# Attention decode kernel (forward and backward): score rows in column strips for the second-batch heads that alternate with second-pass heads

## The chip, the cores and the metric

The kernel runs on one core of a Trainium2 chip. The metric is the device time in microseconds (us), the median of several runs of one program.

## The reference, cut to what matters

Two batch rows, 32 heads, one query token each, a cache of 8192 keys and values of width 128 per head. The forward pass is attention and a gated MLP with adaptive layer norm; the outputs are the result and the gradients of everything, of which dK and dV are by far the largest.

```python
q = (h @ wq).reshape(B, 1, 32, 128).transpose(0, 2, 1, 3)
scores = einsum('bhqd,bhkd->bhqk', q, k_cache) * 128 ** -0.5     # per head: 8192 scores
p = softmax(scores)
o = einsum('bhqk,bhkd->bhqd', p, v_cache)
out = x + gate * (o @ wo) ...                                     # then the MLP
# backward, per head: dV = p (outer) dO ;  dP = V dO ;  dS = p * (dP - sum) ;  dK = dS (outer) q
```

K and V of a head have 2.1 MB each. The kernel reads K once, V twice (once for the output, once for dP), and writes dK and dV: 671 MB of the 709 MB that it moves.

## The kernel before

A head of the *first pass* (A) is: load K and V, transpose K in blocks on TensorE, scores, maximum, exponent, scale K and take the products with V. A head of the *second pass* (C) is: load V again, transpose it, dP, and the two outer products on VectorE, each written out in two halves. Work is laid out in *slots*: a function put at a slot is emitted there, so slots fix the order of instructions on each engine, not the time. There are three stages. Heads 0 to 38 of the first pass follow each other, one per 8 slots (to about 450 us). Then 25 heads of the first pass (39 to 63, second batch) alternate with second-pass heads of the first batch, one pair per 16 slots, about 25 us: the **mixed stage**, up to about 1080 us. Then comes a **passage**, in which the MLP chain of the second batch is worked through, and the remaining second-pass heads, which end the kernel.

```python
    NHALF = 21                                   # big buffers, 1 MB each: half a head's K, V, dK or dV
    def htile():
        return halfp.tile([P, HK, P], BF16, name="half", tag="half")
    ...
    def transposes(block, dve):                  # 8 blocks of 128x128, and the copy out of PSUM
        tp = tps.tile([P, GRP, P], BF16, name="tp", tag="tp")
        for j in range(GRP):
            nc.tensor.transpose(tp[:, j, :], block(j), identb[:])
        kt = ktp.tile([P, GRP, P], BF16, name="kt", tag="kt")
        if dve: nc.vector.tensor_copy(kt[:], tp[:])          # groups 2 and 6
        else:   nc.scalar.copy(kt[:], tp[:])
        return kt

    def a_s(i, g):                               # scores of 8 blocks: K-transposed as weights, q as one column
        b, h = hb(i)
        kt = kts.pop((i, g))
        for j in range(GRP):
            cc = g * GRP + j
            nc.tensor.matmul(S_ps[i][:, cc:cc + 1], kt[:, j, :], qT_bf[:, h, b:b + 1], start=True, stop=True)
    ...
    def job_a(i, s):                             # NG = 8, LAG = 2, MOFF = 15
        for g in range(NG):
            at(s + g, PL_T, lambda g=g: a_t(i, g))
            at(s + g + LAG, PL_S, lambda g=g: a_s(i, g))
            at(s + g + MOFF, PL_M, lambda g=g: a_m(i, g))        # products with V
            at(s + g + MOFF, PL_FREE, lambda g=g: a_free(i, g))  # V halves free
        at(s + NG + LAG, PL_MAX, lambda: a_max(i))
        at(s + NG + LAG + 1, PL_MAX, lambda: a_bias(i))
        at(s + NG + LAG + 2, PL_EXP, lambda: a_exp(i))
        for q in range(NQ):
            at(s + NG + LAG + 3 + 2 * q, PL_TT, lambda q=q: a_scale(i, q))   # VectorE reads K
        ...
        at(s + MOFF + 2, PL_T, lambda: a_kp(i))                  # last matmul that reads K
        at(s + MOFF + 2, PL_FREE, lambda: k_free(i, 0))
        at(s + MOFF + 4, PL_FREE, lambda: k_free(i, 1))
        at(s + MOFF + NG, PL_EV, lambda: a_evac(i))
    ...
    def outer(store, dst, n, which, w2, q):      # dV and dK of the second pass
        hf, o = divmod(q * QK, HK)
        if o == 0:
            free["half"] -= 1
            store[(n, hf)] = htile()             # takes one of the 21 buffers
        ... nc.vector.tensor_tensor(... ALU.mult)
        if o + QK == HK:
            sq_.dma_start(src_of(dst, n)[:, hf * HK:(hf + 1) * HK, :], t[:])   # sq_ = nc.gpsimd
    ...
    # loads: nc.sync queue, in the order of the slot at which they are needed
    want(sA[i] + MOFF + hf * HG, lambda i=i, hf=hf: load_v(i, i, hf))
    ...
    A_END = end_a(sA[NHD - 1])                   # the passage is laid out from here
```

Every big tile takes one of the 21 buffers, and its first writer (a load on the SP queue, or VectorE's outer product) waits until the last user of the tile that was there before is done. The tile framework chooses the buffer when the program is built.

## Time and profile before

| | before |
|---|---|
| time, median of 3 runs | 1744.83 us (1744.82 to 1746.49) |
| bytes moved | 709.31 MB, 407 GB/s over the span |
| mixed stage, 480 to 1080 us | 413 GB/s, DMA share 1.01 |
| TensorE, VectorE, ScalarE busy there | 451.7, 410.5, 308.3 of 600 us |

Read a DMA-bound kernel by its rate, not by the busy share. The share is near 1.0 in nearly every window, at low rates as at high ones. (The Trainium skill, "Perfetto Trace Analysis", Identifying the Most-Contended Engine, says the same: bandwidth instead of occupancy. This trace agrees: a share of 1.01 at 413 GB/s, and still 0.98 at 384.) First, rows of the profile page's second part, 40 equal slices of the span: tenths of DMA's time busy, and GB/s.

```profile
DMA  9999999999999999999999999999999999999997
GB/s 381 417 417 418 418 417 389 418 378 398 375 417 422 418 410 422 411 404 414 409 410 412 420 407 394 369 415 420 425 421 421 410 411 395 417 416 415 410 411 319
```

The windows view of the kernel before follows: window in us; its length; busy us and instructions of TensorE, its weight loads, VectorE, ScalarE and GpSimd; granted clock; DMA share; GB/s.

```profile
20.00:400.00 380.00, 363.83 (x7504) 336.71 (x7505) 239.62 (x387) 228.16 (x321) 122.98 (x203) 0.98 1.01 409
480.00:1080.00 600.00, 451.70 (x8210) 424.66 (x8208) 410.53 (x514) 308.27 (x433) 138.50 (x236) 0.82 1.01 413
1080.00:1160.00 80.00, 63.42 (x1288) 60.18 (x1286) 61.27 (x126) 55.63 (x75) 13.56 (x24) 0.81 0.98 384
1240.00:1700.00 460.00, 346.52 (x4231) 269.61 (x4232) 298.07 (x322) 290.39 (x432) 58.97 (x111) 0.58 1.01 413
```

TensorE is nearly full in the first stage, has a quarter of its time free in the mixed stage, and the passage (third line) moves bytes at the lowest rate. Next, lines of the waits view of the kernel before, 480 to 1080 us: engine and line, for whom it waited, us in total, times, longest.

```profile
DVE half L1101 <- DMA out_dram<-half: 129.8, 23, 8.6
...
PE s_ps L386 <- DVE kt L369: 99.4, 22, 6.6
```

VectorE stood 129.8 us in the mixed stage because the buffer of an output tile was still being sent, and TensorE's score matmuls stood 99.4 us for a copy that VectorE had queued behind. The timeline of VectorE shows it in one period: the start, the length, the instruction, and in brackets the idle time before it and what ended it.

```profile
703.93 1.22 DVE L412 TENSOR_TENSOR ek<-half,e_15747 128x2048 bf16<-128x2048 bf16 x1
711.09 2.36 DVE L1101 TENSOR_TENSOR half<-Qr,ds_15957 128x2048 bf16<-128x2048 bf16 x2 [5.95 <-DMA out_dram<-half]
713.37 0.68 DVE L369 COPY kt<-tp 128x1024 bf16<-128x1024 bf16 x1
```

The first outer product of dK waits 5.95 us for an output transfer, and the copy of transposed K (kt) that TensorE needs comes after it. Last, the SP queue's own waits in that stage: the loads, too, wait for buffers that are being sent.

```profile
SPq L177 <- DMA out_dram<-half: 431.2, 48, 16.5
SPq L171 <- DMA out_dram<-half: 87.6, 22, 4.8
```

### The profile page before, as it was taken

Reading aid. Unit: us, or ns where it says so; the run is one execution under the profiler, and the core shown is the slowest. Engines: PE = TensorE matmul, PEld = TensorE weight load, DVE = VectorE, ACT = ScalarE, POOL = GpSimd, SP = SyncE. Lnnn points to the kernel's source line nnn. Section 1 sums busy time; section 2 is a strip of 40 time slices with the busy share of each in tenths; the row PEclk is TensorE's granted clock in tenths of the full one; section 3 lists DMA queues with packets and bytes.
Section 4 is the critical chain, followed back from the end, with each engine's and each line's share of the span. In section 5 each row is a group of like instructions: output and inputs, shape, how many; then the busy total and the mean of one; then the engine's idle time right before and its main releaser. Section 6 shows DMA issues by size and latency. Waiting matters only on the chain. (4 is left out here: it accounts for less than half of the span.)

```text
span 1743.7 us, 54710 instructions
## 1 busy us (share of the span) xinstructions
PE 1370.3 (79%) x24083; PEld 1221.6 (70%) x24083; DVE 1150.4 (66%) x1595; ACT 1008.0 (58%) x1431; POOL 371.9 (21%) x646
## 2 busy tenths in 40 slices
PE   6999999989967787686787778875577776785883
PEld 5999998879867676676776777875455555564672
DVE  2666666867876576577667668785566666675676
ACT  4666666646555545454454555696456555575784
POOL 0333333322221222222122123111011111110111
PEclk9999999989988878887888788698555556566577
DMA  9999999999999999999999999999999999999997
GB/s 381 417 417 418 418 417 389 418 378 398 375 417 422 418 410 422 411 404 414 409 410 412 420 407 394 369 415 420 425 421 421 410 411 395 417 416 415 410 411 319
DMA packets 109402, 709.31 MB, mean 407 GB/s; under 512 B 11175, under 2 KB 17683, under 8 KB 27243
## 3 DMA queue, kind: packets, MB, share of 16 engines
q1 hardware_dynamic: 67280, 421.59, 59.9%
q0 software_dynamic: 36864, 268.45, 37.0%
q10 hardware_dynamic: 5019, 15.78, 2.3%
q8 instruction: 188, 3.08, 0.7%
q14 instruction: 51, 0.42, 0.1%
HBM read 421.57 MB, written 284.20 MB: 405 GB/s over the span
## 5 line engine op out<-in xcount | busy, mean ns | idle before, releaser
L371 ACT COPY kt<-tp 128x1024 bf16<-128x1024 bf16 x794 | 800.9, 1020 | 546.4 <-PE tp L366 536.4
L366 PE MATMUL tp<-identb,half 128*128 128x128 bf16 x8192 | 772.7, 250 | 19.2 <-DVE kt L369 10.6
L366 PEld LDWEIGHTS <-half 128*128 128x128 bf16 x8192 | 599.8, 113 | 107.7 <-issue 94.6
L1106 POOL DMA_DIRECT2D out_dram<-half x256 | 136.2, 532 | 1034.3 <-DVE half L1101 883.0
L427 PE MATMUL m_ps<-ek,half 128*128 128x129 bf16 x4096 | 328.6, 223 | 1.1 <-DMA half<-in_A_v_cache_dram 1.1
L1078 PE MATMUL s_ps<-DO_bf,kt 128*128 128x1 bf16 x4096 | 192.5, 168 | 109.8 <-DVE kt L369 101.8
L1078 PEld LDWEIGHTS <-kt 128*128 128x128 bf16 x4096 | 186.3, 108 | 125.2 <-DVE kt L369 111.8
L369 DVE COPY kt<-tp 128x1024 bf16<-128x1024 bf16 x230 | 157.9, 686 | 153.6 <-PE tp L366 153.1
L386 PE MATMUL s_ps<-qT_bf,kt 128*128 128x1 bf16 x4096 | 177.7, 164 | 101.3 <-DVE kt L369 99.4
L427 PEld LDWEIGHTS <-half 128*128 128x128 bf16 x4096 | 248.9, 98 | 1.4 <-DMA half<-in_A_v_cache_dram 1.2
L386 PEld LDWEIGHTS <-kt 128*128 128x128 bf16 x4096 | 159.7, 98 | 106.2 <-DVE kt L369 103.6
L1230 ACT CAST stg<-m_ps 128x512 bf16<-128x512 f32 (+2 forms) x124 | 72.4, 584 | 68.5 <-PE m_ps L1229 68.4
L449 PE MATMUL k_ps<-half,pz 128*32 128x512 bf16 x1024 | 68.2, 386 | 23.0 <-POOL pz L435 23.0
L1229 PE MATMUL m_ps<-half 2*128 2x512 bf16 (+2 forms) x124 | 73.8, 595 | 1.2 <-ACT half L1204 1.2
L449 PEld LDWEIGHTS <-pz 128*32 128x32 bf16 x1024 | 21.9, 96 | 45.1 <-POOL pz L435 26.0
L1204 ACT CAST half<-m_ps 2x512 bf16<-2x512 f32 (+1 forms) x36 | 19.9, 564 | 34.9 <-PE m_ps L1201 34.4
L398 DVE TENSOR_REDUCE nm<-s_ps 128x1 f32<-128x128 f32 x64 | 18.4, 287 | 19.4 <-PE s_ps L395 19.4
L395 PE MATMUL s_ps<-nident,rm 128*128 128x128 bf16 x64 | 15.5, 243 | 19.4 <-DVE rm L390 19.4
L1312 ACT COPY kt<-tp 128x1024 bf16<-128x1024 bf16 x28 | 30.1, 1081 | 0.2
L1306 PE MATMUL tp<-identb,half 128*128 128x128 bf16 x224 | 20.3, 245 | 4.7 <-ACT kt L371 4.6
L488 DVE COPY OK<-m_ps 128x1 f32<-128x1 f32 x64 | 9.8, 154 | 20.5 <-ACT half L487 18.8
L729 PE MATMUL s_ps<-d_attn_bf,kt 128*128 128x1 bf16 x256 | 11.2, 165 | 14.8 <-ACT kt L718 12.1
(871 smaller groups left out, 1757.9 us busy)
## 6 DMA issues: line engine op xcount, KB each, us to landing
out_dram<-half POOLq DMA_DIRECT2D x256, 1024.0 KB, 13.7
half<-in_A_v_cache_dram SPq DMA_DIRECT2D x252, 1024.0 KB, 12.4
half<-in_A_k_cache_dram SPq DMA_DIRECT2D x128, 1024.0 KB, 19.6
out_dram<-stg ACTq DMA_DIRECT2D x22, 512.0 KB, 10.0
half<-in_A_wq_dram SPq DMA_DIRECT2D x8, 1024.0 KB, 10.2
half<-in_A_wo_dram SPq DMA_DIRECT2D x4, 1024.0 KB, 20.5
half<-in_w_mod_dram SPq DMA_DIRECT2D x3, 1024.0 KB, 15.9
half<-in_B_w_dram SPq DMA_DIRECT2D x3, 1024.0 KB
```

The source lines that it names most:

```text
L366: nc.tensor.transpose(tp[:, j, :], block(j), identb[:])
L369: nc.vector.tensor_copy(kt[:], tp[:])
L371: nc.scalar.copy(kt[:], tp[:])
L386: nc.tensor.matmul(S_ps[i][:, cc:cc + 1], kt[:, j, :], qT_bf[:, h, b:b + 1], start=True, stop=True)
L427: nc.tensor.matmul(m[:, 0:P + 1], vb_(i, kk), t[:, kk % QK, 0:P + 1], start=(kk == 0), stop=(kk == KK - 1), skip_group_check=True)
L449: nc.tensor.matmul(kp["ps"][NR * j:NR * (j + 1), :], pz[:, o:o + NR], K[(i, kk // HK)][:, kk % HK:kk % HK + QP, :], start=False, stop=(h = ...
L1078: nc.tensor.matmul(DP[n][:, cc:cc + 1], kt[:, j, :], DO_bf[:, b, h:h + 1], start=True, stop=True)
L1106: sq_.dma_start(src_of(dst, n)[:, hf * HK:(hf + 1) * HK, :], t[:])
L1229: nc.tensor.matmul(ps[:lw, 0:rw], rsl(ln, lc, lw, step), rsl(rn, rc, rw), start=True, stop=True)
L1230: nc.scalar.copy(st["t"][:lw, o:o + rw], ps[:lw, 0:rw])
L1306: nc.tensor.transpose(tp[:, j, :], rows[kc][:, (m0 + j) * P:(m0 + j + 1) * P], identb[:])
L1312: nc.scalar.copy(kt[:], tp[:])
```

## The change

The score matmuls of the 25 alternating heads are turned around. Instead of K-transposed as weights and the query as a single moving column (64 weight loads and 64 one-column matmuls a head), the query becomes the weights, padded with zeros so that one column of a 32-column strip holds it, and K-transposed moves, 512 columns at a time, in four strips side by side: 16 matmuls a head. The scores then stand in rows; ScalarE copies them out and four fp32 matmuls turn them into the columns that softmax wants. To make room, everything after the scores but the last copy of the outputs comes one slot later for these heads, and the stage that follows is laid out one slot later.

```diff
+    ssel = cst.tile([P, NSL * NST], F32, name="ssel")            # picks rows back into columns
+    qz = [cst.tile([P, NR + NSL - 1], BF16, name=f"qz{k}") for k in range(NZ)]   # zeros around q
...
     def a_t(i, g):
         if g == 0:
-            S_ps[i] = head_ps()
+            if i in byrows:
+                nc.gpsimd.tensor_copy(qz[i % NZ][:, NSL - 1:NSL], qT_bf[:, h, b:b + 1])
+            else:
+                S_ps[i] = head_ps()
...
+    def a_srow(i, g):
+        if g % SG < SG - 1:
+            return
+        a = g // SG
+        if a == 0:
+            R_ps[i] = mtps()
+        w = qz[i % NZ][:, NSL - 1 - a:NSL - 1 - a + NR]
+        for j in range(NST):
+            kt = kts[(i, g - SG + 1 + j * SW // GRP)]
+            o = j * SW % GRP
+            nc.tensor.matmul(R_ps[i][NR * j:NR * (j + 1), :], w, kt[:, o:o + SW, :],
+                             start=(a == 0), stop=(a == NSL - 1))
+    def a_rows(i):
+        t = ekp.tile([P, SW * P], F32, name="srow", tag="ek")
+        nc.scalar.copy(t[:], R_ps.pop(i)[:])
+    def a_cols(i):
+        S_ps[i] = head_ps()
+        for c in range(SW):
+            nc.tensor.matmul(sv[:, c, :], t[:, c * P:(c + 1) * P], ssel[:], start=True, stop=True)
...
     def job_a(i, s):
+        x = 1 if i in byrows else 0
+        MOFF = moff(i)                                            # MOFF + 1 for byrows
-        at(s + NG + LAG, PL_MAX, lambda: a_max(i))
+        if x:
+            at(s + NG + LAG, PL_EXP, lambda: a_rows(i))
+            at(s + NG + LAG + 1, PL_EXP, lambda: a_cols(i))
+        at(s + NG + LAG + x, PL_MAX, lambda: a_max(i))            # bias, exp, scale likewise + x
...
+    byrows.update(i for i in range(NHD) if sA[i] >= E0)           # heads 39 to 63
-    A_END = end_a(sA[NHD - 1])
+    A_END = end_a(sA[NHD - 1]) + 1
-            want(sA[i] + MOFF + hf * HG, ...load_v)
+            want(sA[i] + moff(i) + hf * HG, ...load_v)
```

Left out: the copy of one output column moves from VectorE to ScalarE for these heads, and two small uses of PSUM (the memory that matmuls write to) move to another bank, since the strips need one.

**What the diff does not say.** The later slot changes the moment at which K's buffers are given back, and with it the framework's choice of buffers. By the two built programs, ten big tiles take their buffers in each period of the mixed stage as follows (in 16 to 21 of 21 periods; 0 and 1 are halves; W is V loaded again for the second pass):

```
new tile   takes the buffer of, before      takes the buffer of, after
dK0        dV1  (an output transfer)        K0   (read last by TensorE)     <- swapped
V1         K0   (read last by TensorE)      dV1  (an output transfer)       <- swapped
W0 <- dK0   V0 <- dK1   K0 <- dV0   K1 <- V0   dV0 <- V1   dV1 <- W0   dK1 <- K1   W1 <- W1   in both
```

Below, this table is called the *handover*.

More of the change, by code (lines that the diff above doesn't have):

```diff
@@ L123 @@
     nc.vector.memset(pz[:], 0.0)
+    SW = 512 // P
+    NSL = KK // (SW * NST)
+    SG = SW * NST // GRP
+    ssel = cst.tile([P, NSL * NST], F32, name="ssel")
+    nc.vector.tensor_copy(ssel[:].rearrange("p (x j) -> p x j", j=NST),
+                          identb[:].rearrange("p (j x) -> p x j", j=NST)[:, 0:NSL, :])
+    NZ = 3
+    qz = [cst.tile([P, NR + NSL - 1], BF16, name=f"qz{k}") for k in range(NZ)]
+    for z in qz:
+        nc.vector.memset(z[:], 0.0)
     rsum = cst.tile([P, NHD], F32, name="rsum")
@@ L355 @@
     S_ps = {}
+    R_ps = {}
     M_ps = {}
@@ L376, in a_t @@
     def a_t(i, g):
+        b, h = hb(i)
         if g == 0:
-            S_ps[i] = head_ps()
+            if i in byrows:
+                nc.gpsimd.tensor_copy(qz[i % NZ][:, NSL - 1:NSL], qT_bf[:, h, b:b + 1])
+            else:
+                S_ps[i] = head_ps()
         kts[(i, g)] = transposes(lambda j: kb_(K, i, g * GRP + j), g in (2, 6))
+    byrows = set()
+    def a_srow(i, g):
[10 more added lines that the diff above has]
+                             start=(a == 0), stop=(a == NSL - 1))
+        for k in range(SG):
+            kts.pop((i, g - k))
+    def a_rows(i):
+        t = ekp.tile([P, SW * P], F32, name="srow", tag="ek")
+        nc.scalar.copy(t[:], R_ps.pop(i)[:])
+        kts[("row", i)] = t
+    def a_cols(i):
+        S_ps[i] = head_ps()
+        t = kts.pop(("row", i))
+        sv = S_ps[i][:, 0:KK].rearrange("p (m c) -> p c m", c=SW)
+        for c in range(SW):
+            nc.tensor.matmul(sv[:, c, :], t[:, c * P:(c + 1) * P], ssel[:], start=True, stop=True)
     def a_s(i, g):
+        if i in byrows:
+            return a_srow(i, g)
         b, h = hb(i)
@@ L487, in a_evac @@
         nc.scalar.copy(mstate[b][:, h, :], m[:, 0:P])
-        nc.vector.tensor_copy(OK[:, i, 0:1], m[:, P:P + 1])
+        if i in byrows:
+            nc.scalar.copy(OK[:, i, 0:1], m[:, P:P + 1])
+        else:
+            nc.vector.tensor_copy(OK[:, i, 0:1], m[:, P:P + 1])
     def job_a(i, s):
+        x = 1 if i in byrows else 0
+        MOFF = moff(i)
         for g in range(NG):
@@ L495, in job_a @@
             at(s + g + MOFF, PL_FREE, lambda g=g: a_free(i, g))
-        at(s + NG + LAG, PL_MAX, lambda: a_max(i))
-        at(s + NG + LAG + 1, PL_MAX, lambda: a_bias(i))
-        at(s + NG + LAG + 2, PL_EXP, lambda: a_exp(i))
+        if x:
+            at(s + NG + LAG, PL_EXP, lambda: a_rows(i))
+            at(s + NG + LAG + 1, PL_EXP, lambda: a_cols(i))
+        at(s + NG + LAG + x, PL_MAX, lambda: a_max(i))
+        at(s + NG + LAG + x + 1, PL_MAX, lambda: a_bias(i))
+        at(s + NG + LAG + x + 2, PL_EXP, lambda: a_exp(i))
         for q in range(NQ):
-            at(s + NG + LAG + 3 + 2 * q, PL_TT, lambda q=q: a_scale(i, q))
+            at(s + NG + LAG + x + 3 + 2 * q, PL_TT, lambda q=q: a_scale(i, q))
         at(s + MOFF, PL_EXP, lambda: a_pz(i))
@@ L507, in job_a @@
             at(s + MOFF + 4, PL_M, lambda: a_kp_out(i))
-        at(s + MOFF + NG, PL_EV, lambda: a_evac(i))
+        at(s + MOFF + NG - x, PL_EV, lambda: a_evac(i))
     def take_m(b):
@@ L512, in take_m, with moff @@
         free["half"] -= 1
+    def moff(i):
+        return MOFF + (1 if i in byrows else 0)
     def end_a(s):
@@ L1013 @@
         s += NG
-    A_END = end_a(sA[NHD - 1])
+    byrows.update(i for i in range(NHD) if sA[i] >= E0)
+    R0 = min([sA[i] for i in byrows], default=sA[NHD - 1])
+    A_END = end_a(sA[NHD - 1]) + 1
     CS1 = A_END + 1
@@ L1039 @@
                 want(sA[i] + hf * HG, lambda i=i, hf=hf: load_k(i, hf))
-            want(sA[i] + MOFF + hf * HG, lambda i=i, hf=hf: load_v(i, i, hf))
+            want(sA[i] + moff(i) + hf * HG, lambda i=i, hf=hf: load_v(i, i, hf))
     for b in range(B):
@@ L1081, in c_spread @@
         b, h = hb(n)
-        ps = mtps()[:, 0:2 * P]
+        ps = scr(2 * P) if R0 <= now[0] <= A_END else mtps()[:, 0:2 * P]
         nc.tensor.matmul(ps[:, 0:P], Qr_bf[:, b, h:h + 1].to_broadcast((P, P)), identb[:], start=True, stop=True)
@@ L1154, in task_dq @@
     def task_dq(b):
-        ps = mtps()
+        ps = scr(H)
         bs = slice(b * H, (b + 1) * H)
```

## The prediction

> **What bounds the kernel.** The page's DMA row is at 9 tenths in all slices but the last (7), 709.31 MB at 407 GB/s. The windows view splits it: first-batch stage (20-400 us) 409 GB/s, TensorE busy 363.8; mixed stage (480-1080 us, where a second-batch head alternates with a second-pass head) 413 GB/s, DMA share 1.01, TensorE busy only 451.7 of 600, VectorE 410.5, ScalarE 308.3; passage (1080-1160) 384; last stage 413. Windows of 4 us reach 424 to 432 GB/s at best. So the DMA engines bound the mixed stage, and TensorE has about a quarter of it idle: the waits view gives 99.4 us of score matmuls waiting for VectorE's copy, which itself stood 129.8 us behind output transfers whose buffers it needed.
>
> **What it removes and adds**, for 25 heads (39 to 63):
> - TensorE: 64 single-column score matmuls a head go (in the timeline, 8 advance it 0.21 us at full clock, so 1.7 us a head, 42 us in all). Added: 16 matmuls 128x512 into 32-row strips. k_ps has the form: 386 ns each, but 16 in about 1.0 us (the Trainium skill, "TensorE: Matmul & The Clock Gate", Part 3, says distinct column groups run concurrently; the trace agrees), and four fp32 matmuls (8 such take 0.86 us now), 0.4 us. Net gain, an estimate: 0.3 us a head, 8 us of idle engine.
> - ScalarE: one 128x512 copy (592 ns, as kprow) and the OK copy: about 0.75 us a head, 19 us. VectorE loses 25 x 0.157 = 4 us. One slot more lies between scores and outputs, so K is held longer.
>
> **The larger effect is indirect.** Comparing the buffer assignment of the two built programs: before, the first output tile of each second-pass head in the mixed stage reuses a buffer whose output transfer was issued six allocations ago, so VectorE blocks (5.95 and 6.74 us in two periods), TensorE stalls about 5 us, then all runs in a burst, after which the rate drops to 315-401 GB/s for some 4-8 us. After, that tile takes the buffer of a K half freed by TensorE; the waits for output transfers go to loads on the SP queue. VectorE's waits for output transfers in the mixed stage should nearly vanish, TensorE's stall with it; SP's wait for them should grow.
>
> The bytes are the same, all queues share the same 16 DMA engines (the Trainium skill, "Trainium Kernel Development and Optimization", Key Constraints), and their share is full, so unblocking VectorE can only fill the dips. At 424 GB/s throughout, the mixed stage would be 600 x (1 - 413/424) = 16 us shorter. I take under half: -7 us, and +1 us for the later slot.
>
> **Predicted: 1738 us; 8 in 10 between 1722 and 1752. Faster by over 2%: 5%; within 2%: 92%; slower by over 2%: 3%.**
>
> **Signs.** Right: mixed stage still DMA share about 1.01, at 415 to 420 GB/s; VectorE waits for output transfers in that stage under 40 us (129.8); TensorE's waits on VectorE's kt under 40 us; strips matmul 16 in about 1.0 us; last stage unchanged within 3 us. Wrong: DMA share under 0.98 in the mixed stage, or TensorE waiting for loads at over 2 us a period.
>
> **What would make it wrong.** (a) Loads now stand in order behind output transfers; if they come late, DMA starves and the stage is 1 us a period slower, +24 us. (b) A head's last scale now stands between the halves of the first output tile and delays it by 1.2 us. (c) The dips vanish wholly: -16 us, and more with the passage (7 us to give).

## The result, and the profile after

The changed kernel took 1746.25 us (median of 4 runs, 1743.93 to 1747.08) beside 1745.16 us before (1744.82 to 1746.49). The ratio is 1.0003, with a 95% interval of 0.9985 to 1.002. A ratio is the mean time of one kernel's runs over that of the other's in the same rounds, so it is not quite the ratio of the medians. A second set of five rounds on another chip gave a ratio of 1.0000 (0.9987 to 1.0013). There is no gain.

The lines of the profile after that answer to those above: first the page's rows.

```profile
GB/s 381 416 416 416 417 416 388 416 380 394 366 409 424 424 424 417 422 396 421 424 405 424 407 424 381 372 407 422 425 422 414 417 403 396 406 414 414 405 414 319
```

Then the windows view of the changed kernel, the same stages.

```profile
20.00:400.00 380.00, 364.08 (x7463) 337.33 (x7464) 238.14 (x383) 226.89 (x319) 123.36 (x203) 0.97 1.01 407
480.00:1080.00 600.00, 479.44 (x7314) 414.65 (x7314) 416.63 (x491) 319.94 (x483) 88.87 (x258) 0.85 1.01 415
1080.00:1160.00 80.00, 69.21 (x1269) 65.97 (x1268) 61.00 (x124) 54.52 (x75) 12.62 (x23) 0.70 0.99 380
1240.00:1700.00 460.00, 340.44 (x4194) 265.47 (x4194) 294.11 (x318) 290.03 (x432) 57.92 (x109) 0.58 1.01 411
```

The mixed stage is at 415 GB/s in place of 413; the passage is at 380 in place of 384 and the last stage at 411 in place of 413. Next, the waits view of the changed kernel in the mixed stage.

```profile
PE tp L377 <- DMA half<-in_A_k_cache_dram: 67.2, 25, 7.2
...
PE s_ps L423 <- ACT srow L415: 25.2, 24, 1.1
...
DVE half L1160 <- DMA out_dram<-half: 3.4, 1, 3.4
```

VectorE's 129.8 us behind output transfers are 3.4 us, as forecast. TensorE now waits 67.2 us for loads of K, 25 times, which the prediction had named as a sign against it if it came to more than 2 us a period; over the 24 periods it came to 67.2 / 24 = 2.8 us. The second line belongs to the new work: 25.2 us of TensorE standing for ScalarE's row copy. The loads on the SP queue wait for output transfers somewhat less than before, 472.8 us in place of 518.8, where the prediction had said that this should grow:

```profile
SPq L187 <- DMA out_dram<-half: 370.7, 68, 15.7
SPq L181 <- DMA out_dram<-half: 102.1, 22, 5.0
```

The timelines of VectorE and then TensorE of the changed kernel, in a comparable period. VectorE goes through the outer product of dK without a wait, with a head's last scale (ek) between its two halves. On TensorE, four strips take 0.34 us until the next instruction (0.33 to 0.34 in this period); the four fp32 matmuls are eight instructions, 0.91 us, after 1.05 us of waiting for the row copy; and a transpose waits 5.49 us for K.

```profile
704.25 1.22 DVE L1160 TENSOR_TENSOR half<-Qr,ds_15547 128x2048 bf16<-128x2048 bf16 x1
705.39 1.22 DVE L458 TENSOR_TENSOR ek<-half,e_15376 128x2048 bf16<-128x2048 bf16 x1
706.52 1.22 DVE L1160 TENSOR_TENSOR half<-Qr,ds_15547 128x2048 bf16<-128x2048 bf16 x1
```

```profile
709.48 0.40 PE L408 MATMUL m_ps<-kt,qz_108 128*32 128x512 bf16 x4
709.82 0.62 PE L377 MATMUL tp<-identb,half 128*128 128x128 bf16 x8
...
711.67 1.06 PE L423 MATMUL s_ps<-ssel,srow 128*128 128x16 f32 x8 [1.05 <-ACT srow L415]
712.58 0.61 PE L377 MATMUL tp<-identb,half 128*128 128x128 bf16 x8
...
722.36 1.04 PE L377 MATMUL tp<-identb,half 128*128 128x128 bf16 x8 [5.49 <-DMA half<-in_A_k_cache_dram]
```

So in TensorE's own order a head costs it more than before, not less: minus 8 x 0.21 = 1.7 us, plus 4 x 0.33 = 1.3 us of strips, 0.9 us of turning and 1.05 us of waiting.

**Where the trace gains and loses.** Adding up the rates of 4 us windows gives the time at which a trace has moved a given number of bytes. The table shows that time for the kernel before, and how much earlier (negative) or later the others are. The columns to the right of the first two are from experiments told below; each column is one execution, the profiled one. That of the kernel before took 1745.59 us, 1.2 to 2.9 us more than its medians beside the experiments (1742.67 to 1744.39), so the leads look larger by about that much than they are in the kernel's time. A second trace with the handover of before (e_double, below) stands 1.3 us ahead at 420 MB and 1.4 at 700.

| MB moved | before, us | changed | changed, second profile | best version | p_late | k_late |
|---|---|---|---|---|---|---|
| 200 (early in the mixed stage) | 496.8 | +2.9 | +0.3 | +0.8 | +1.2 | +1.5 |
| 320 | 785.8 | +1.0 | -3.1 | -3.9 | -4.1 | -3.3 |
| 420 (way into the passage) | 1028.8 | -2.3 | -7.7 | -7.6 | -7.8 | -6.1 |
| 460 | 1132.0 | -2.1 | -6.2 | -5.9 | -4.0 | -2.9 |
| 500 | 1227.6 | -0.9 | -5.1 | -5.3 | -4.2 | -2.7 |
| 700 (near the end) | 1711.2 | +1.5 | -4.3 | -4.2 | -2.1 | -2.6 |

The first profile of the changed kernel gained 5.2 us between 200 and 420 MB, but lost 2.9 us on the way in and 3.8 us on the way out. Its second profile, from the fastest of five runs (1741.09 us; the other four took 1743.8 to 1745.4), reached the forecast 7 us by the end of the mixed stage and gave back 3.4 us of it. The gain is in the mixed stage; the question is what takes it back.

### The profile page after: what moved, and what is told of

Its sections match the earlier page's. It is cut to its first block, busy times and chain, and to the rows that moved or that the text cites. A ratio compares the mean times of both kernels' runs of the same rounds, so it can differ in the third digit from the quotient of the medians.

```text
span 1745.0 us, 52735 instructions
## 1 busy us (share of the span) xinstructions
PE 1403.7 (80%) x23083; PEld 1216.6 (70%) x23083; DVE 1155.7 (66%) x1574; ACT 1018.3 (58%) x1481; POOL 318.7 (18%) x671
## 4 chain that ended last, share of the span: by engine, by line
issue 30%; PE 30%; DMA 28%; POOL 4%; DVE 4%; ACT 2%; SPq 1%; POOLq 0%; ACTq 0%; DVEq 0%
DMA half<-in_A_k_cache_dram 19%; PE tp L377 12%; PE m_ps L473 9%; DMA out_dram<-half 6%; POOL out_dram L1165 4%; PE k_ps L495 2%; PE s_ps L432 2%; DVE ek L458 2%; DVE half L1160 1%; DMA half<-in_w_mod_dram 1%; ACT kt L382 1%; PE m_ps L408 1%; DMA half<-in_A_wo_dram 1%; PE s_ps L423 1%; DMA half<-in_A_v_cache_dram 1%
## 5 line engine op out<-in xcount | busy, mean ns | idle before, releaser
L377 PE MATMUL tp<-identb,half 128*128 128x128 bf16 x8192 | 753.8, 247 | 79.1 <-DMA half<-in_A_k_cache_dram 69.0
L473 PE MATMUL m_ps<-ek,half 128*128 128x129 bf16 x4096 | 342.5, 228 | 4.0 <-DVE ek L458 2.3
L1137 PEld LDWEIGHTS <-kt 128*128 128x128 bf16 x4096 | 180.3, 106 | 122.0 <-DVE kt L380 105.5
L432 PE MATMUL s_ps<-qT_bf,kt 128*128 128x1 bf16 x2496 | 107.6, 164 | 1.0 <-DVE lnst L1020 0.4
L432 PEld LDWEIGHTS <-kt 128*128 128x128 bf16 x2496 | 96.8, 97 | 1.7 <-issue 1.0
L423 PE MATMUL s_ps<-ssel,srow 128*128 128x16 f32 x200 | 27.4, 269 | 25.2 <-ACT srow L415 25.2
L423 PEld LDWEIGHTS s_ps<-ssel,srow 128*128 128x128 f32 x200 | 24.9, 195 | 27.3 <-ACT srow L415 27.3
L1365 PE MATMUL tp<-identb,half 128*128 128x128 bf16 x224 | 20.4, 245 | 13.4 <-DVE kt L380 8.8
```

Source lines behind the costliest of these rows:

```text
L423: nc.tensor.matmul(sv[:, c, :], t[:, c * P:(c + 1) * P], ssel[:], start=True, stop=True)
L473: nc.tensor.matmul(m[:, 0:P + 1], vb_(i, kk), t[:, kk % QK, 0:P + 1], start=(kk == 0), stop=(kk == KK - 1), skip_group_check=True)
L1137: nc.tensor.matmul(DP[n][:, cc:cc + 1], kt[:, j, :], DO_bf[:, b, h:h + 1], start=True, stop=True)
```

## The experiments

Sixteen kernels were run in four sets; in each, the kernels shared a chip and the runs of the kernel before. The theories, at the outset: **A**, the dips in the mixed stage come from the handover of buffers, and the changed handover is worth some microseconds, which something else in the change costs again; **B**, the transfers cannot do better in that mix, so there was nothing to gain; and **C**, TensorE's time counts, and the strips cost what the handover gains.

### What the transfers alone can do

```diff
-    (all compute; this cut is shortened, four writes of zeros are left out)
+    def head_c(n):
+        for hf in range(2):
+            t = load(A_v_cache, n, hf)          # nc.sync, 21 buffers
+            store(t, out_3, n, hf)              # nc.gpsimd, from the loaded tile
+            store(t, out_2, n, hf)
+    for i in range(39): head_a(i)               # head_a loads K and V
+    for k in range(25): head_c(k); head_a(39 + k)
+    for n in range(25, 64): head_c(n)
```

> The big transfers alone (671 of the 709 MB: K, V, V again, and two outputs per head sent from the loaded V tile), in the same order of heads, through the same queues and 21 buffers, no compute, a wrong result on purpose. If the dips below 424 GB/s in the mixed stage come from how the engines hand over buffers (theory A, that of the prediction), this holds about 424 GB/s in every stage: 671.1 MB / 424 GB/s = 1583 us, and no stage below 420. If the transfers themselves cannot do better in the mix of reads and writes (rival B: nothing was there to gain), its mixed stage shows about 413 to 416 GB/s as in both kernels and the whole takes about 1620 us.

Measured: 1600.56 us (2 runs; of the small outputs only some zeros are written). The windows view of this run, its three stages, with busy time of VectorE and GpSimd only:

```profile
20.00:390.00 370.00, 0.00 (x0) 0.00 (x0) 1.00 1.01 422
400.00:1010.00 610.00, 0.00 (x0) 51.62 (x98) 1.00 1.01 427
1010.00:1580.00 570.00, 0.00 (x0) 82.85 (x156) 1.00 1.01 421
```

In the mix of the second stage the transfers run at 427 GB/s, against 413 and 415 in the two kernels: 600 x (1 - 413/427) = 20 us were there to gain at most. Theory B falls for that stage. Whether the engines' own reading and writing of the tiles, absent here, takes a part of the 20 us was not tested. (The Trainium skill, "HBM Reference", Specifications, gives about 425 GB/s to a core that streams alone; 422 for reads only here agrees roughly, and the mix does slightly better.) In the last stage the transfers alone come to 421 GB/s on average and both kernels are at 411 to 413, so less is left there. The larger gap lies at the passage: from 1080 to 1160 us the transfers alone are still at 427 GB/s, the two kernels at 384 and 380. The forecast of 420 everywhere held; the total of 1583 us did not: it left out the slower start and end (170 GB/s in the first 4 us, 225 and less in the last 12) and took 424 for every stage.

### Does TensorE's time count?

```diff
-            nc.tensor.matmul(S_ps[i][:, cc:cc + 1], kt[:, j, :], qT_bf[:, h, b:b + 1], start=True, stop=True)
+            for _ in range(2 if sA[i] >= E0 else 1):
+                nc.tensor.matmul(S_ps[i][:, cc:cc + 1], kt[:, j, :], qT_bf[:, h, b:b + 1], start=True, stop=True)
```

> The kernel before, with each of the 64 score matmuls of heads 39 to 63 issued twice (1600 more matmuls, some 42 us of TensorE at full clock). If TensorE is off the critical path in the mixed stage, the time stays within 3 us of before. If TensorE time counts there, it grows by 20 to 42 us, and then the removal of the same matmuls in the change should have gained.

Measured: 1746.99 us beside 1743.86, ratio 1.0017 (1.0003 to 1.003). The windows view of the mixed stage shows that the added work was done, at an almost unchanged rate:

```profile
480.00:1080.00 600.00, 484.07 (x9734) 455.08 (x9732) 410.49 (x514) 309.09 (x434) 137.88 (x235) 0.84 1.01 412
```

TensorE is busy 32 us more than before. The 1600 matmuls, with the handover of before, cost 3 us and not 20 to 42. Score matmuls of TensorE are nearly free in that stage, so removing them could gain little.

### The later slot alone, and the strips alone

The slot alone: the kernel before with `x`, `moff(i)` and the `A_END + 1` of the change, and its own column scores. Its handover is that of the changed kernel. The strips alone: the changed kernel with these lines back (the cut leaves out the last copy of the outputs, whose slot stays the same). Maximum, bias and exponent stay one slot later, since the rows must be turned first.

```diff
-        MOFF = moff(i)
-            at(s + NG + LAG + x + 3 + 2 * q, PL_TT, lambda q=q: a_scale(i, q))
+            at(s + NG + LAG + 3 + 2 * q, PL_TT, lambda q=q: a_scale(i, q))
-        return MOFF + (1 if i in byrows else 0)
+        return MOFF
-    A_END = end_a(sA[NHD - 1]) + 1
+    A_END = end_a(sA[NHD - 1])
```

> The kernel before with its column scores, but with the timing of the change alone: maximum, exponent, scale and outputs of heads 39 to 63 one slot later. The built program hands buffers over as in the changed kernel (VectorE's output tiles no longer reuse buffers that wait for an output transfer). Theory A1: the handover is worth 3 to 7 us and the strips cost it again, so this is 3 to 7 us faster than before. Rival: the handover only moves waits (TensorE then waits for K loads) and the time stays within 2 us of before.

> The changed kernel's strips without the later slot for the outputs: the scores are taken by strips and turned, and the outputs stay at the slots of before; VectorE's output tiles again wait for output transfers. Theory A1 (the strips cost TensorE time where it is on the path, at the entry to the mixed stage, and the handover gains it back): 2 to 6 us slower than before. Rival: strips cost nothing, within 2 us of before.

Measured: the slot alone 1744.81 us (1739.72 to 1746.7), ratio 0.9997 (0.9984 to 1.0011): no gain, although its trace was 7.3 us ahead at 420 MB. The strips alone 1757.67 us (1756.92 to 1761.25), ratio 1.008 (1.0066 to 1.0094): 14 us slower, far more than either theory had said. By its built program the framework had chosen a third handover there: W0 takes W0's buffer and dV1 takes dK0's, so that two of VectorE's four output tiles wait for transfers. Its waits view in the mixed stage, VectorE and then the SP queue, and its windows view:

```profile
DVE half L1159 <- DMA out_dram<-half: 110.6, 41, 8.4
```

```profile
SPq L187 <- PE tp L377: 336.5, 50, 12.7
```

```profile
480.00:1080.00 600.00, 488.86 (x7120) 421.85 (x7119) 401.87 (x478) 310.08 (x463) 115.26 (x253) 0.81 1.01 405
```

Loads stood 336.5 us for a transpose that had to release the buffer, and the stage ran at 405 GB/s. Either the strips cost 14 us or this handover does. That cannot be told from these two runs, since each edit also moved the buffers.

### Choosing the handover by hand

To tell them apart, the buffers were taken out of the framework's hands: 21 pools of one buffer each, and a table that names the buffer of every big tile. The table is read from another built program. Instructions and their order stay as they are; the framework still puts in every wait.

```diff
-    halfp = ctx.enter_context(tc.tile_pool(name="halfp", bufs=NHALF))
+    halfs = [ctx.enter_context(tc.tile_pool(name=f"half{k}", bufs=1)) for k in range(NHALF)]
-        return halfp.tile([P, HK, P], BF16, name="half", tag="half")
+        return halfs[HMAP[key]].tile([P, HK, P], BF16, name="half", tag="half")
+    HMAP = {("K", 0, 0): 19, ("K", 0, 1): 18, ...}     # 664 entries
```

h_swap is the kernel before with the table of the slot-only kernel; h_back the changed kernel with the table of the kernel before; h_strips the strips-alone kernel with the table of the slot-only kernel. e_20 is a check of another kind: `NHALF = 20`.

> The kernel before, instruction for instruction, but each big tile is put by hand into the buffer that it had in the slot-only kernel. In the mixed stage this swaps two of ten handovers: the first dK tile takes the buffer of the K half that TensorE has freed (it was that of dV's second output transfer), and the second V load waits for that transfer instead. Theory A1 (the handover is worth 7 us in the mixed stage, and the later slot, which holds K longer, or something after it takes this back): VectorE's wait for output transfers there falls from 130 us to under 15 us, and the time is 3 to 8 us under before. Rival (the handover only moves the wait): within 2 us.

> The changed kernel, instruction for instruction, but each big tile in the buffer that it had in the kernel before. Theory A1 (strips and later slot cost about as much as the handover gains): VectorE waits for output transfers again (over 90 us in the mixed stage) and the time is 3 to 10 us over before. Rival (handover, strips and slot are all free of effect): within 2 us of before.

> The kernel with strips and the old slots, which was 14 us slower than before, with its big tiles put by hand into the buffers of the slot-only kernel. If its 14 us came from its handover (two of VectorE's four output tiles and a load behind transfers, SP waiting 336 us for transposes), they go: within 3 us of before. If they came from the strips' own work, it stays 10 to 16 us slower.

> The kernel before with 20 big buffers in place of 21; by the built programs 10 of them circulate in the mixed stage in place of 11. If that stage is held by the number of buffers (the transfers alone reach 427 GB/s there), it loses about a tenth of the in-flight work and the time grows by 20 to 60 us, all of it after 400 us... the first-batch stage, which has more free buffers, loses less than 3 us. If buffers are plentiful, the time stays within 4 us.

| run | time, us | beside before, us | ratio (95% interval) |
|---|---|---|---|
| h_swap | 1740.93 (1740.27 to 1741.35) | 1744.3 | 0.9980 (0.9967 to 0.9994) |
| h_back | 1795.15 (1791.28 to 1798.62) | 1744.3 | 1.0290 (1.0276 to 1.0304) |
| h_strips | 1741.56 (1738.2 to 1742.36) | 1744.3 | 0.9979 (0.9966 to 0.9993) |
| e_20 | 1751.8 (2 runs) | 1744.3 | 1.0042 (1.0023 to 1.006) |

Four things follow.

The other table alone, with every instruction of the kernel before, gains 0.2%, 3.5 us (h_swap). In 104 of its 664 entries the tile follows another tile in its buffer than in the kernel before: 46 of these are the swap, 12 an exchange of V0 and W1 in six periods, and 46 lie at the end of the mixed stage or after it. The trace puts the gain before those last 46 (0.6 us ahead at 200 MB, 5.7 at 420, 4.6 at 700); the exchange in six periods was not separated from the swap. The waits view of h_swap in the mixed stage shows the same exchange as the changed kernel: VectorE no longer waits, TensorE waits for K.

```profile
PE tp L377 <- DMA half<-in_A_k_cache_dram: 65.1, 25, 4.4
...
DVE half L1112 <- DMA out_dram<-half: 2.8, 2, 1.4
```

The strips cost nothing: with that handover they are at 0.9979, without them at 0.9980. The 14 us of the strips-alone kernel were its handover. With e_double this removes theory C.

The changed kernel with the handover of before is 51 us slower (h_back), five times the upper end of what was expected. The waits and the windows view of that run say why:

```profile
DVE half L1171 <- DMA out_dram<-half: 119.0, 22, 8.5
...
PE m_ps L484 <- DVE ek L469: 103.5, 20, 8.4
```

```profile
480.00:1080.00 600.00, 433.98 (x6794) 369.11 (x6791) 383.04 (x451) 297.20 (x446) 81.50 (x242) 0.87 0.98 387
```

One slot later, a head's last scale comes after the first outer product of dK on VectorE. When that outer product waits for a transfer, the scale waits behind it (in one period of this trace the outer product starts at 700.72 us, after 5.90 us of waiting, and the scale at 701.86), and TensorE's products with V wait for the scale, 103.5 us in all. The stage falls to 387 GB/s. That V's buffers then come free late, and the loads with them, is the likely link; the SP queue's waits do not show it, since they come to 541 us in the mixed stage as against 545 before. So with the later slot the old handover would have cost 51 us. The framework's choice of the new one saved the change, and that was luck: nobody had asked for it.

With ten circulating buffers in place of 11 the kernel loses 0.4%, 7.5 us, under the 20 to 60 expected. This run is no clean test of the number, because the program built with 20 buffers has a handover of its own (K0 takes K0's buffer, V1 takes V0's). Its trace is 0.5 us ahead of before at 420 MB and 7.6 us behind at 460: the loss falls on the way into the passage, none of it in the mixed stage. (The Trainium skill, "Perfetto Trace Analysis", Optimization Strategy, says that equal gaps repeating on the engine that should be saturated can mean too few buffers. Here the repeated dips were mended in part, 413 to 415 GB/s from 480 to 1080 us in h_swap, at an equal number of buffers.)

### With and without the later slot, on one chip

> The changed kernel once more, on the chip of the three below, so that they can be compared with it there: within 3 us of before, as its first four runs were (+0.5 us by the ratio).

> The changed kernel with its big tiles put by hand into the buffers of the slot-only kernel; that differs from its own choice in two periods of the mixed stage. If these odd periods cost it the gain, it is 3 to 5 us under before. If the later slot costs the gain (theory now), it stays within 2 us of the changed kernel.

> The candidate that beat both: strips, outputs at the old slots, the same handover as the run above it; so it differs from that run only in the later slot. Theory: 2 to 5 us under before again, and at least 2 us under the changed kernel with the same handover. If it is within 1 us of that one, the later slot costs nothing and the difference seen between chips was chance.

> The slot-only kernel with its own handover, but the last three heads at the old slots, so that the stage that follows is laid out where it was before. The slot-only kernel led by 7.3 us at 420 MB in its trace and lost 3 to 5 us of it by 500 MB. If the later slot costs at this passage, this keeps the lead: 3 to 6 us under before. If it costs in every period, or not at the passage, it is 0 to 2 us under before.

"best" is h_strips once more: strips, the old slots, the new handover. h_mid is the slot-only kernel with the last three heads and `A_END` at the old slots.

| run | time, us | ratio to before (95% interval) |
|---|---|---|
| after_again (the changed kernel) | 1744.56 (1741.09 to 1745.41) | 1.0000 (0.9987 to 1.0013) |
| h_after (the same, handover by hand) | 1745.19 (1742.35 to 1745.98) | 1.0001 (0.9989 to 1.0012) |
| best (h_after without the later slot) | 1740.11 (1739.32 to 1742.14) | 0.9976 (0.9964 to 0.9988) |
| h_mid | 1743.53 (1736.68 to 1747.8) | 0.9992 (0.9974 to 1.0009) |

The pair h_after and best differs only in the later slot: (1.0001 - 0.9976) x 1744 = 4.4 us, clear of the noise (the slowest of five runs of best took 1742.14 us, the fastest of h_after 1742.35). The later slot takes back what the handover gains. The odd periods of the changed kernel's own handover cost nothing that can be seen, nor do the 21 pools in place of one (h_after is as after_again). h_mid scattered over 11 us and decides nothing. The best version beats the kernel before in two sets on two chips, by 0.21 and 0.24%, and the changed kernel in the one set in which both ran.

### Which part of the later slot?

Four more kernels, all with the new handover by hand. p_late: best with only `A_END + 1`. p_early: the changed kernel with `A_END` back. k_late: best with only the last reading of K and K's release one slot later. m_late: best with only the products with V and V's release one slot later.

```diff
 p_late   +    A_END = end_a(sA[NHD - 1]) + 1
 p_early  -    A_END = end_a(sA[NHD - 1]) + 1     (back to end_a(sA[NHD - 1]))
 k_late   +        at(s + MOFF + 2 + x, PL_T, lambda: a_kp(i))       # and both k_free + x
 m_late   +            at(s + g + MOFF + x, PL_M, lambda g=g: a_m(i, g))   # and a_free + x
```

> The best version (strips, old slots, new handover) with only the stage after the mixed one laid out one slot later. If the later slot costs at this hand-on, it gives back 2 to 4 us of the best version's lead: 0 to 2 us under before. If not, 3 to 5 us under before, as the best version.

> The changed kernel with the new handover and the later slot, but the stage after the mixed one laid out where it was before. If the hand-on is what costs, 2 to 4 us under before. If not, within 1.5 us of before, as with the hand-on one slot later.

> The best version with only the row of K products and the release of K one slot later for heads 39 to 63. If holding K longer is what costs, it gives back 2 to 4 us: 0 to 2 us under before. If not, 3 to 5 us under before.

> The best version with only the output products and the release of V one slot later for heads 39 to 63. If it is the outputs' later slot that costs, it gives back 2 to 4 us: 0 to 2 us under before. If not, 3 to 5 us under before.

| run | time, us | beside before, us | ratio (95% interval) |
|---|---|---|---|
| p_late | 1743.3 (1741.82 to 1745.67) | 1742.67 | 1.0001 (0.9988 to 1.0014) |
| p_early | 1742.84 (1740.86 to 1743.33) | 1742.67 | 0.9994 (0.9982 to 1.0007) |
| k_late | 1742.45 (1740.54 to 1743.39) | 1742.67 | 0.9993 (0.9981 to 1.0006) |
| m_late | 1740.55 (1738.58 to 1741.43) | 1742.67 | 0.9980 (0.9967 to 0.9994) |

The outputs' later slot costs nothing that can be seen (m_late keeps the lead of best). The version best itself was not run in this set; m_late stands in for it. Against m_late, laying the passage out one slot later costs 3.7 us by the ratios (3.3 by the plain means) and so takes the whole lead by itself (p_late, 1.0001). Holding K one slot longer costs 2.3 us (2.0 by the plain means; k_late, 0.9993), which is less certain: its interval overlaps that of m_late. Undoing the passage alone recovers only 1 us (p_early), within the noise. So the parts do not add up. Two more parts, the last scale and the loads of V one slot later, were not varied by themselves. The windows view shows where p_late loses, mixed stage and then the way into the passage; the version "best" is given first, then p_late.

```profile
480.00:1029.00 549.00, 441.89 (x6734) 375.66 (x6734) 380.46 (x448) 292.88 (x441) 120.66 (x242) 0.86 1.01 420
1029.00:1132.00 103.00, 85.70 (x1509) 78.42 (x1506) 75.08 (x128) 59.56 (x90) 18.05 (x32) 0.77 0.96 378
```

```profile
480.00:1029.00 549.00, 436.26 (x6736) 367.85 (x6734) 379.94 (x449) 292.45 (x441) 121.17 (x242) 0.88 1.01 420
1029.00:1132.00 103.00, 83.46 (x1443) 77.09 (x1441) 72.65 (x125) 57.66 (x86) 18.04 (x32) 0.75 0.96 372
```

Both run the mixed stage at 420 GB/s. In the 103 us after it p_late moves 372 GB/s and best 378, about 0.6 MB less, or 1.6 us. By the table above the two are 1.9 us apart at 460 MB and 2.1 at 700, so nearly all that these two traces differ by arises there. In one trace each, that is an indication, not a proof: p_early, with the passage at the old slots, loses as much on the way in (6.4 us ahead at 420 MB, 2.1 at 460). Why one slot matters at the passage, when the DMA rate there is so low for all of them, stays open.

## Why the prediction was right or wrong

- *DMA bounds the mixed stage, TensorE has time to spare there.* Right. TensorE's score matmuls twice over cost 3 us (e_double), and the strips cost nothing at an equal handover.
- *The larger effect is the handover.* Right, and it is more than an effect: with the change's instructions the two handovers are 51 us apart (h_back beside before, h_after at 1.0001), and with the instructions of before, the new handover gains 3.5 us (h_swap).
- *VectorE's waits for transfers vanish, TensorE's stall on VectorE's copy with them.* Right: 129.8 to 3.4 us, and 99.4 us to nothing for the score matmuls. But *SP's wait for them should grow* was wrong: 518.8 to 472.8 us. The wait that came in its place is TensorE's for K, 67.2 us.
- *At 424 GB/s the stage would be 16 us shorter; "I take under half: -7 us".* The mechanism was right, the size held for the stage and not for the kernel. Of twelve profiles taken with the new handover, eleven stood 5.7 to 7.8 us ahead of before at 420 MB, the first profile of the changed kernel only 2.3 us. In the kernel's time the handover is worth 3.5 to 4.2 us (h_swap, h_strips, best). A part of the lead is lost after 420 MB, not at the same place in every version: best is 7.6 us ahead at 420 MB, 5.3 at 500 and 4.2 at 700; h_swap loses nothing on the way into the passage (5.7 at 420 and at 460 MB) and ends at 4.6. Why is not shown.
- *"and +1 us for the later slot".* This is the step that failed most. Measured on one chip, the later slot costs 4.4 us (h_after against best). The prediction priced it as 1 us. Two parts of it cost more than that, each alone: the passage laid out a slot later (3.7 us, p_late against m_late by their ratios) and K held a slot longer (2.3 us, k_late against m_late, less certain). The prediction named the second ("K is held longer") and priced neither.
- The sum, -3.5 to -4 us of handover, about 0 of strips, and +4.4 us of slot, is the measured zero. The two mis-sized terms, -7 and +1, each make up about half of the 6 us by which the forecast was off.
- *TensorE's net gain of 0.3 us a head.* Wrong in sign, without consequence: a head costs TensorE 1.6 us more in its own order, because the four fp32 matmuls are eight instructions and wait for the row copy. The forecast of 0.4 us for the four took "8 such take 0.86 us" from the kernel before, but those 8 were the instructions of four matmuls: 0.86 us was the figure for four, and 0.91 was measured. The 16 strips, forecast at 1.0 us, take 1.3 in groups of four.
- *Wrong if TensorE waits for loads over 2 us a period.* It did (2.8 us), and this was no sign of a slower stage: h_swap waits as long (65.1 us) and is faster. In h_swap the wait moved from VectorE to TensorE, and the kernel gained by it.

What stays open: how one slot at the passage, or K held one slot longer, costs what it does; why the mixed stage ran at 417 GB/s from 480 to 1029 us in the first profile of the changed kernel and at 420 in the second; why p_late and k_late do not add up; and where the remaining 7 GB/s to the 427 of the transfers alone are lost in the mixed stage, and 40 GB/s at the passage.

## What to carry to other kernels

In a kernel that is bound by transfers, ask of every tile whose buffer it takes: in the kernel before, VectorE stood 129.8 us for buffers that were still being sent, and with it the copies queued behind, for which TensorE stood 99.4 us. With the wait at a load instead, TensorE stood 65.1 us for K, and the kernel was 3.5 us faster (h_swap). A shift by one slot can change this choice without a line of the diff saying so, so read the buffers out of the built program, and to learn what an edit costs, fix the buffers by hand and vary one thing at a time. A gain in one stage counts only as far as the stages after it keep the lead: of 7.6 us at the end of the mixed stage, best kept 4.2.

## What the Trainium skill lacked or had wrong

- "Perfetto Trace Analysis", Optimization Strategy, names too little room (buffer count, tile sizes) as a possible cause of repeated bubbles. It lacks another cause: which tile inherits which buffer. With instructions unchanged and 21 buffers throughout, a changed assignment moved the kernel by -0.2% (h_swap) and by +2.9% (h_back), while one buffer fewer, with the other handover that came with it, cost 0.4% (e_20).
- "HBM Reference", Specifications, gives about 425 GB/s for a core streaming alone and does not speak of mixes. The transfers alone came to 422 GB/s for reads, 427 for three reads to two writes, and 421 on average for one read to two writes (427 up to 1160 us, 412 to 423 after).
- "TensorE: Matmul & The Clock Gate", Part 3, says that column tiles run concurrently, and this holds for the strips here: 401 to 413 ns on average for one of them, but four in 0.33 us. The page does not say into how many instructions an fp32 matmul is split: with 128 weight columns and 16 moving ones, 100 such were recorded as 200, 0.91 us for four.
